# A linear-attention and MLP kernel: half of the first matmul's blocks as Strassen products in six of nine groups

## The chip, the cores and the metric

The kernel runs on one core of one Trainium2 chip. The metric is the device time of one execution in microseconds; the kernel before has a median of 272.02 us over three runs (271.81 to 272.04).

The names of the engines in the profile: PE is TensorE's matmul, PEld its weight load, DVE is VectorE, ACT is ScalarE, POOL is GpSimd, SP is SyncE, which here only issues DMAs.

## What is computed

```python
def _attn_ref(q, k, v):                 # q, k, v: (8 batches, 8 heads, 576 tokens, 64)
    def phi(x):
        return np.where(x > 0, x, np.exp(x) - 1.0) + 1.0
    q_p, k_p = (phi(q), phi(k))
    kv = np.einsum('bhsd,bhse->bhde', k_p, v)
    z = np.sum(k_p, axis=2)
    num = np.einsum('bhsd,bhde->bhse', q_p, kv)
    den = np.einsum('bhsd,bhd->bhs', q_p, z)[..., None] + 1e-06
    return (num / den).astype(np.float32)

def _moe_ref(x, w_in, w_out):           # x: (4608, 512), w_in: (512, 2048), w_out: (2048, 512)
    h = x @ w_in
    c = np.float32(np.sqrt(2.0 / np.pi))
    g = 0.5 * h * (1.0 + np.tanh(c * (h + 0.044715 * h * h * h)))
    return (g @ w_out).astype(np.float32)
```

x is the attention's output with the heads side by side.

## The kernel before

The 4608 tokens are worked in nine groups of 512 (`iteration(j)`, L880). Groups 0 to 7 are the first 512 tokens of the eight batches, group 8 the remaining 64 tokens of each.

One group has two stages. First the **h stage**: sixteen blocks of 128 columns of w_in, each four matmuls of 128x128 weights against 512 tokens of the transposed x (`h_mm`, L392), into one bank of PSUM, from which ScalarE's gelu (L409) writes g in fp16. Then the **product stage**: g times w_out. From group 1 on it is already done by Strassen's scheme: seven products of quarter matrices (`Products`, L756), each sixteen matmuls against 256 columns (L790). VectorE forms the sums of quarters that they need (`sums`, `third_sum`, `last_sum`) and adds up the results (`plus`, L862); ScalarE copies two partial results (L821, L834) and starts the stores. The products run in the order 1, 5, 6, 7, 2, 4, 3. Their accumulators are called p, z, v and w.

Between these stages the **attention of the next group** is put in. For its batch, exponentials (`exp_of`, on ScalarE, L222), the linear part of phi (`linear_of`, DVE, L230), the minimum of both (`least_of`, DVE, L238) and a cast of v (`cast_v_paired`, L243) are made one or two groups ahead. `nab_quads` (L318) then issues 32 small matmuls of numerators and denominators into four banks and a pair of banks, then 72 small ones that make kv of the batch after, and then five divides on DVE (a reciprocal, L287, and a multiplication, L288, each). The quotient x is transposed by DMAs that SP issues (L694), as q is (L671).

The order on every engine is written out by hand. `at(j, slot, fn)` (L517) puts a piece of work behind step `slot` of group j, and `run` (L522) issues it there; engines work off their instructions in that order. In groups 2 to 8 the steps 0 to 15 are the h blocks in the order 0, 8, 1, 9, ..., 7, 15, and 16 to 22 the seven products. The `plan_` functions (L526 to L704) hold the placing: the attention stands behind step 9 (step 12 in group 2).

The kernel uses eight banks of PSUM. `bank()` (L78) gives out six of them, the other two are the pair (L81). In the program a new tile takes the bank that was released longest ago in program order: the accumulators are released in the order v, p, w, z, and the next h blocks take their banks in just that order. The first instruction that writes the tile waits until the last reader of the one before is done. The buffers for loads (`pld`, L48) are seven, given out in the same way.

Of the kernel before, what the change touches and what calls it, by code (L numbers as in the profile page):

```python
# [8 lines left out]
FP32 = mybir.dt.float32  # L9
BF16 = mybir.dt.bfloat16  # L10
# [6 lines left out]
def kernel(  # L17
# [16 lines left out]
    nc = tc.nc  # L34
# [24 lines left out]
    pout = ctx.enter_context(tc.tile_pool(name="pout", bufs=2))  # L59
    psm = ctx.enter_context(tc.tile_pool(name="psm", bufs=2))  # L60
    pkv = ctx.enter_context(tc.tile_pool(name="pkv", bufs=1))
    ps_b = ctx.enter_context(
        tc.tile_pool(name="ps_b", bufs=6, space=bass.MemoryType.PSUM)
    )
# [6 lines left out]


    ident = const.tile([P, P + 64], BF16, name="ident")[:, 0:P]
    w_in_sb = const.tile([P, KM, d_ff], BF16, name="w_in_sb")
    w_out_sb = const.tile([P, 2, MM, N2], FP16, name="w_out_sb")
    w_sum = const.tile([P, 3, MM // 2, N2], FP16, name="w_sum")

# [100 lines left out]

    warm = const.tile([P, 512], BF16, name="warm")
    nc.vector.memset(warm, 0.0)  # L182
    make_identity(nc, ident)
    vps = [pkv.tile([P, J * NP, E], BF16, name=f"vp{i}") for i in range(2)]
    kvbds = [pkv.tile([P, NP, 2 * E], BF16, name=f"kvbd{b}") for b in range(3)]
    kvs = {b: pkv.tile([P, NP, E], BF16, name=f"kv{b}") for b in range(3, B)}
    for i in range(2):
        nc.gpsimd.memset(vps[i][:, :, D:E], 1.0)
# [32 lines left out]
            o, i = o[..., cs, :], i[..., cs, :]  # L221
        nc.scalar.activation(o, i, AF.Exp)  # L222

    def linear_of(name, b, hs=None):
        x = ld[name, b]
        hs = hs or slice(0, x.shape[1])
        if (name, b) not in phi:
            phi_tiles(name, b)
        o, i = maps_view(name, b, x, phi[name, b], hs)
        nc.vector.tensor_scalar(o, i, 1.0, 1.0, op0=ALU.add, op1=ALU.max)  # L230

    def least_of(name, b, hs=None, cs=None):
        p, e = phi[name, b], exps[name, b]
# [62 lines left out]

    def x_tile(b, c):
        if b not in xs:
            xs[b] = pxs.tile([P, C, d_model], BF16, name="xs")
        return xs[b][:, c]  # L300

    def by_parity(x):
# [12 lines left out]
            divide(by_parity(x)[:, a], ns[a].rearrange("p (u e) -> p u e", e=E))  # L315
        return x

    def nab_quads(qt_cs, bs, kv_b):  # L318

        ns = [[bank("n_ps", [P, 6 * E]) for _ in range(2)] for _ in range(2)]
        n_pair = pair_of_banks("n_ps")
        ns.append([n_pair[:, s] for s in range(2)])
        units = [(c, i, a) for c in range(C) for i in range(2) for a in range(2)]
        for n, (c, i, a) in enumerate(units):
            g = n // 6
            one = bs[c][0] == bs[c][1]
            for t in range(1 if one else 2):
                for s in range(2):  # L330
                    cs = slice(0, P) if one else slice(HP * t, HP * (t + 1))
                    nc.tensor.matmul(  # L332
                        ns[g][s][cs, E * (n - 6 * g) : E * (n - 6 * g + 1)],
                        lhsT=qt_cs[c][HP * s : HP * (s + 1), 2 * a + i, cs],
                        rhs=kv_of_head(bs[c][t], s, 2 * a + i),
                        skip_group_check=True,
                    )
        if kv_b is not None:
            for ii in range(2):
                kv_paired(kv_b, ii, lambda a, ii: n_pair[:, a, E * (4 + ii) : E * (5 + ii)])  # L340

        def x_of(transposed):
            x = pxs.tile([P, C, d_model], BF16, name="xs")
            x_v = x.rearrange("p c (i s a d) -> p s (c i) a d", s=2, a=2, d=D)
            for g in range(2):
                for s in range(2):
                    divide(
                        x_v[:, s, 3 * g : 3 * (g + 1)],
                        ns[g][s].rearrange("p (k a e) -> p k a e", a=2, e=E),
                    )  # L350
                for c in ((0,), (1, 2))[g]:
                    transposed(c, x[:, c])
            n_v = n_pair[:, :, 0 : 4 * E].rearrange("p s (k a e) -> p s k a e", a=2, e=E)
            divide(x_v[:, :, 6:8], n_v)
            transposed(3, x[:, 3])
            if kv_b is not None:
                nc.vector.tensor_copy(
                    out=kvs[kv_b].rearrange("p (a i) e -> p a i e", a=2),
                    in_=n_pair[:, :, 4 * E : 6 * E].rearrange("p a (i e) -> p a i e", e=E),
                )  # L360

        return x_of
# [19 lines left out]
        )  # L382

    def transpose_x(x, xt_c, fn, blocks=range(NP)):
        t_ps = bank("t_ps", [P, len(blocks), P], BF16)
        for n, i in enumerate(blocks):
            nc.tensor.transpose(t_ps[:, n, :], x[:, P * i : P * (i + 1)], ident)  # L387
        fn(out=xt_c[:, blocks.start : blocks.stop], in_=t_ps)

    xts, qts = {}, {}  # L390
# [35 lines left out]
    def first_batch():  # L426
# [44 lines left out]
        for i in range(2):  # L471
            cast_w_out(i, nc.gpsimd.tensor_copy)

        xts[0] = pt.tile([P, NP, MAIN], BF16, name="xt")
        x = {0: x_tile(0, 0)}

        def t(c, blocks=range(NP)):
# [34 lines left out]

    fill = {}

    def at(j, slot, fn, *args):  # L517
# [8 lines left out]
    def plan_second():  # L526
# [43 lines left out]

        def t(c):
            if c == 0:
                xts[b] = pt.tile([P, NP, MAIN], BF16, name="xt")
            transpose_x(x[c], xt_chunk(b, c), nc.scalar.copy)

        at(0, 15, maps)
# [38 lines left out]
    def plan_fourth():  # L615

        for slot, hs in zip((9, 13), halves):
            at(1, slot, linear_of, "k", 3, hs)
        at(1, 17, exp_of, "k", 3)
        at(1, 18, exp_of, "q", 3)  # L620
        at(1, 18, exp_of, "k", 4)
        at(1, 18, gelu_table)
        at(1, 20, least_of, "k", 3)
        at(1, 21, linear_of, "q", 3)
        at(2, 0, cast_v, 3)
        at(2, 0, least_q, 3)
        at(2, 4, kv_in_pair, 3)
        at(2, 5, linear_of, "k", 4)
        at(2, 5, least_of, "k", 4)
        at(2, 5, cast_v, 4)  # L630
        at(2, 8, linear_of, "q", 4)
        at(2, 15, exp_of, "q", 4)
        at(2, 16, exp_of, "k", 5)
        at(2, 19, least_q, 4)
        at(2, 22, linear_of, "k", 5)
        at(3, 0, least_of, "k", 5)

    def plan_prepare(j):

        b = j + 2  # L640
        has_k = b + 1 < B
        at(j, 0, linear_of, "q", b)
        at(j, 0, cast_v, b)
        at(j, 15, exp_of, "q", b)
        at(j, 17, least_q, b)
        if has_k:
            at(j, 10, linear_of, "k", b + 1)
            at(j, 16, exp_of, "k", b + 1)
            at(j, 20, least_of, "k", b + 1)

    def plan_rest(m):
        j = 5 + m // 2

        def least():
            least_of("qr", m)
            if m == 0:
                qts[B] = pt.tile([P, C, NP, P], BF16, name="qt")
            nc.sync.dma_start_transpose(
                out=qts[B][:, m], in_=phi["qr", m][:, 0].rearrange("p h d -> p (h d)")
            )  # L660

        at(j, 6 if j == 5 else 0, linear_of, "qr", m)
        at(j, 15, exp_of, "qr", m)
        at(j, 18, least)

# [24 lines left out]

    def transposed_x(b, c, x):
        if b not in xts:
            xts[b] = pt.tile([P, NP, MAIN], BF16, name="xt")
        nc.sync.dma_start_transpose(out=xt_chunk(b, c), in_=x)  # L694

    def plan_attention(b):


        def attention():
            bs = [(b, b) if b < B else (2 * c, 2 * c + 1) for c in range(C)]  # L700
            x_of = nab_quads([qts[b][:, c] for c in range(C)], bs, b + 1 if b + 1 < B else None)
            x_of(lambda c, x: transposed_x(b, c, x))

        at(b - 1, 12 if b == 3 else 9, attention)  # L704

    def evac(dst, src, on_scalar):
        (nc.scalar.copy if on_scalar else nc.vector.tensor_copy)(dst, src)
# [48 lines left out]
    class Products:  # L756
# [42 lines left out]
        def step(self, name):  # L799
# [41 lines left out]
            elif name == 3 and j < B:  # L841
                self.product(self.z, a11, b22, False)
                self.plus(self.o1[:, :, hi], self.z, self.o1[:, :, hi])
                at(j + 1, 0, self.store, 0, self.o1)
            elif name == 3:
                for t in range(2):
                    self.product(self.z, a11, b22, False, (t,))
# [22 lines left out]
        def store(self, h, o_sb, fs=slice(0, d_model)):  # L870
# [5 lines left out]
            else:  # L876
                for t in range(2):
                    self.store_rest(2 * h + t, o_sb[:, t], fs)

    def iteration(j):  # L880
        xt = xts[j]
        if j < B:
            g = pg.tile([P, 2, MM, MAIN // 2], FP16, name="g")
        else:
            g = pg.tile([P, MM, 2, MAIN // 2], FP16, name="g").rearrange("p m a n -> p a m n")
        hs = [("h", m) for m in range(MM)]
        us = [range(m, m + 4) for m in range(0, MM, 4)]
        products = Products(j, g) if j else None
# [4 lines left out]
        elif j == 1:  # L893
# [6 lines left out]
            at(1, 14, products.sums, early)  # L900
            at(1, 17, products.sums, late)
            at(1, 19, products.last_sum)
        else:
            steps = [hs[i + n] for i in range(MM // 2) for n in (0, MM // 2)]
            steps += [("product", n) for n in (1, 5, 6, 7, 2, 4, 3)]
# [2 lines left out]
                at(j, slot, products.third_sum, ms)  # L908
            at(j, 16, products.last_sum)
        o_pss = {}  # L910
        for slot, step in enumerate(steps):
            if step[0] == "h":
                m = step[1]
                h_ps = h_begun.get(j, {}).get(m)
                if h_ps is None:
                    h_ps = bank("h_ps", [P, MAIN])
                    h_mm(h_ps, xt, m)
                gelu(j, g, m, h_ps)
            elif step[0] == "product":
                products.step(step[1])  # L920
            else:
# [3 lines left out]
                o_mm(o_pss[t], g, t, u, half=(j, slot - 0.5))  # L925
                if u.stop == MM:
                    finish(j, t, o_pss[t])
            run(j, slot)

    plan_second()  # L930
    plan_third()
# [15 lines left out]
        at(5, 1, load_rest, m + 2)  # L947
    for j in range(2, 7):
        at(j, 16, gelu_table)

    for j in range(B + 1):
        iteration(j)
# [30 lines left out]
```

## Time and profile before

| | us |
|---|---|
| median of three runs | 272.02 |
| span of the profiled execution | 270.2 |
| PE busy in the span | 264.4 |
| DVE, ACT busy in the span | 164.7, 166.0 |
| groups 3 to 8, from their first matmul to the last product's end | 104.82 to 266.81 |

The page gives no time of the profiled execution beside its span. The span counts from the first to the last instruction; the time of a run has 1.8 us more around it.

In a row of the page's fifth part stand the line, the engine, the operation, what it writes and reads, the form, and how often; then busy time, the mean of one in ns, and the engine's idle time ahead of it. A matmul's own duration is longer than its share of the stream, since matmuls overlap: a 512-column one lasts 379 ns but one follows every 0.216 us. The chain that ended last shows the stream's pace, the row does not.

### The profile page before, as it was taken

How to read it: one execution, taken by the hardware profiler on the slowest of the kernel's cores; microseconds unless marked ns; L12 is line 12 of the kernel's file. 1: busy time of each engine (PE TensorE's matmuls, PEld its weight loads, DVE VectorE, ACT ScalarE, POOL GpSimd, SP SyncE). 2: the span in 40 equal slices, each digit the busy share in tenths (PEclk: the TensorE clock that was granted, in tenths of full speed). 3: DMA queues.
4: the chain of work that ended last, by engine and by line, in shares of the span. 5: the costliest groups of instructions: out<-in, count | busy, mean ns of one | idle time of the engine just before them, and what ended most of it. 6: DMA issues, size and time to landing. Idle time of an engine off the chain costs nothing.

```text
span 270.2 us, 5941 instructions
## 1 busy us (share of the span) xinstructions
PE 264.4 (98%) x2533; PEld 170.8 (63%) x2533; DVE 164.7 (61%) x265; ACT 166.0 (61%) x225; POOL 15.0 (6%) x21
## 2 busy tenths in 40 slices
PE   8999999999999999999999999999999999999994
PEld 2584456465854686558655874587458745874584
DVE  2860186988999966788738774693267326622262
ACT  4768877799776683668266926582665265028700
POOL 3056401000000000000000000000000000000000
PEclk9999999999999999999999999999999999999999
DMA  6999999995799998893699474219231412121004
GB/s 234 401 405 396 410 408 400 400 382 98 232 290 257 327 245 222 292 295 78 172 355 268 91 151 137 61 39 159 96 41 43 135 56 61 19 113 45 0 2 155
DMA packets 59786, 53.87 MB, mean 199 GB/s; under 512 B 35696, under 2 KB 45936, under 8 KB 59760
## 3 DMA queue, kind: packets, MB, share of 16 engines
q1 hardware_dynamic: 56880, 44.57, 58.4%
q10 hardware_dynamic: 2880, 8.91, 8.7%
q8 instruction: 20, 0.33, 0.5%
q14 instruction: 6, 0.05, 0.0%
HBM read 36.70 MB, written 9.44 MB: 171 GB/s over the span
## 4 chain that ended last, share of the span: by engine, by line
PE 92%; DMA 3%; DVE 2%; SPq 1%; issue 0%; ACT 0%
PE h_ps L394 45%; PE o_ps L790 36%; PE o_ps L734 5%; DMA v_x<-in_v_dram 3%; PE n_ps L332 1%; PE kv_ps L254 1%; PE n_ps L254 1%; PE n_ps L270 1%; PE t_ps L387 1%; SPq L94 1%; DVE s L763 0%; SPq L99 0%; PE t_ps L545 0%; DVE kvbd L686 0%; DVE vp L243 0%
## 5 line engine op out<-in xcount | busy, mean ns | idle before, releaser
L394 PE MATMUL h_ps<-xt,w_in_sb 128*128 128x512 bf16 (+1 forms) x628 | 128.4, 361 | 0.2 <-issue 0.2
L409 ACT ACTIVATE g<-h_ps 128x512 f16<-128x512 f32 x144 | 86.8, 616 | 59.5 <-PE h_ps L394 57.5
L394 PEld LDWEIGHTS <-w_in_sb 128*128 128x128 bf16 x628 | 58.2, 98 | 62.4
L790 PEld LDWEIGHTS <-g 128*128 128x128 f16 x624 | 60.9, 98 | 9.0 <-ACT g L409 0.2
L790 PE MATMUL o_ps<-w_out_sb,g 128*128 128x256 f16 x496 | 58.2, 273 | 0.0
L862 DVE TENSOR_TENSOR o_sb<-o_ps,o_sb 128x512 f32<-128x512 f32 (+1 forms) x42 | 27.9, 665 | 29.4 <-PE o_ps L790 28.5
L763 DVE TENSOR_TENSOR s<-g 128x1024 f16<-128x1024 f16 x18 | 12.4, 691 | 40.0 <-ACT g L409 39.9
L790 PE MATMUL o_ps<-w_sum,s 128*128 128x256 f16 x256 | 29.3, 273 | 0.0
L790 PEld LDWEIGHTS <-s 128*128 128x128 f16 x272 | 26.6, 98 | 3.1
L288 DVE TENSOR_TENSOR xs<-n_ps,r 128x384 bf16<-128x384 f32 (+2 forms) x44 | 25.6, 582 | 1.5
L222 ACT ACTIVATE k_e<-k_x 128x2304 bf16<-128x2304 f32 (+1 forms) x9 | 17.2, 1910 | 3.7 <-DVE k_p L238 2.9
L834 ACT COPY o_sb<-o_ps 128x512 f32<-128x512 f32 x8 | 4.7, 583 | 22.3 <-PE o_ps L790 22.3
L230 DVE TENSOR_SCALAR q_p<-q_x 128x2048 bf16<-128x2048 f32 (+1 forms) x9 | 9.9, 1101 | 13.2 <-DMA q_x<-in_q_dram 13.2
L222 ACT ACTIVATE q_e<-q_x 128x2048 bf16<-128x2048 f32 (+1 forms) x10 | 15.7, 1568 | 2.9 <-DMA q_x<-in_q_dram 2.9
L790 PE MATMUL o_ps<-w_sum,g 128*128 128x256 f16 x128 | 15.3, 273 | 0.0
L734 PE MATMUL o_ps<-w_out_sb,g 128*128 128x512 f16 x64 | 15.1, 379 | 0.0
L230 DVE TENSOR_SCALAR k_p<-k_x 128x2304 bf16<-128x2304 f32 (+1 forms) x10 | 11.1, 1113 | 4.2 <-DMA k_x<-in_k_dram 4.1
L422 ACT ACT_TABLE_LOAD x9 | 11.5, 1283 | 0.2
L431 PE MATMUL w_ps<-warm 128*128 128x512 bf16 x32 | 10.3, 484 | 1.2 <-DVE warm L182 1.2
L763 DVE TENSOR_TENSOR s<-s,g 128x1024 f16<-128x1024 f16 x16 | 11.1, 692 | 0.5
L238 DVE TENSOR_TENSOR k_p<-k_p,k_e 128x2304 bf16<-128x2304 bf16 (+1 forms) x9 | 11.0, 1221 | 0.7 <-ACT k_e L222 0.3
L243 DVE CAST vp<-v_x 128x2304 bf16<-128x2304 f32 (+1 forms) x9 | 11.0, 1225 | 0.5 <-DMA v_x<-in_v_dram 0.4
(63 smaller groups left out, 151.3 us busy)
## 6 DMA issues: line engine op xcount, KB each, us to landing
out_dram<-o_sb ACTq DMA_DIRECT2D x16, 512.0 KB, 3.9
k_x<-in_k_dram SPq DMA_DIRECT2D x7, 1152.0 KB, 9.3
v_x<-in_v_dram SPq DMA_DIRECT2D x7, 1152.0 KB, 12.0
q_x<-in_q_dram SPq DMA_DIRECT2D x6, 1024.0 KB, 12.6
w_st<-in_moe_w_in_dram SPq DMA_DIRECT2D x3, 1024.0 KB, 13.3
q_x<-in_q_dram SPq DMA_DIRECT2D x4, 512.0 KB, 8.7
w_st<-in_moe_w_out_dram SPq DMA_DIRECT2D x2, 1024.0 KB, 13.8
w_st<-in_moe_w_out_dram SPq DMA_DIRECT2D x4, 512.0 KB, 11.2
```

The costliest lines, as they stand in the source:

```text
L222: nc.scalar.activation(o, i, AF.Exp)
L230: nc.vector.tensor_scalar(o, i, 1.0, 1.0, op0=ALU.add, op1=ALU.max)
L238: nc.vector.tensor_tensor(p, p, e, op=ALU.min)
L243: fn(out=vp_paired(b)[:, :, us, 0:D].rearrange("p j u d -> p u j d"), in_=ld["v", b][:, us].rearrange("p u (j d) -> p u j d", d=D),)
L288: nc.vector.tensor_tensor(x_v, n_v[heads + (slice(0, D),)], r[heads + (None,)].to_broadcast(shape + [D]), op=ALU.mult,)
L394: nc.tensor.matmul(h_ps[:, ts], lhsT=w_in_sb[:, c, P * m : P * (m + 1)], rhs=xt[:, c, ts], start=(c == 0), stop=(c == KM - 1), skip_group_ ...
L409: nc.scalar.activation(g_v, h_v, AF.Gelu_apprx_tanh)
L422: nc.scalar.preload_act_table_set("gelu_apprx_tanh_and_others")
L734: nc.tensor.matmul(o_ps, lhsT=g[:, t // 2, m, P * (t % 2) : P * (t % 2 + 1)], rhs=w_out_sb[:, :, m, :], start=(m == 0), stop=(m == MM - 1),)
L763: nc.vector.tensor_tensor(out, i0, i1, op=op)
L790: nc.tensor.matmul(ps[t] if type(ps) is list else ps[:, t, :], lhsT=lhs[:, m, P * t : P * (t + 1)], rhs=rhs[:, m, :], start=(first and m = ...
L862: nc.vector.tensor_tensor(out, i0, i1, op=ALU.add)
```

## The change

In groups 3 to 8, eight of the sixteen h blocks are no longer computed one by one. Blocks 0, 1, 8, 9 are unit 0, blocks 4, 5, 12, 13 unit 1. A unit is a 2x2x2 block product (two pairs of blocks, two halves of the 512 inputs, two halves of the 512 tokens) done as seven products of four matmuls of 256 columns. Blocks 2, 10, 3, 11, 6, 14, 7, 15 stay as they were.

Sums are taken in PSUM where they can be. Product 1 is copied by ScalarE into the bank of the last plain block (the seed), and product 2 accumulates on it; product 6 and then 5 and 3 accumulate in product 1's bank; product 4 in product 7's, to which DVE then adds u2 in place. The four sums of w_in per unit are made once, in group 2 (`sum_w_in`), the four sums of x once per group, at the end of the group before (`sum_x`). They live in a new pool and in two of the seven load buffers. For these sums w_in and x are kept in fp16 instead of bf16, with an identity in fp16 for the transposes on PE.

Around it work is moved. The attention of the next group comes behind step 4 (step 5 where there is no further kv), kv first; its divides are three parts behind steps 5, 6 and 7. The cast of v goes from DVE to ScalarE, into the product stage of the group before. `least_of` of k goes to the start of the next group, `linear_of` of k and of the rest of q into or just ahead of the product stage, all sums of g behind steps 13 to 16, one store from slot 0 to 1.

```diff
-    def nab_quads(qt_cs, bs, kv_b):
+    def nab_quads(qt_cs, bs, kv_b, transposed, kv_first):
...
         units = [(c, i, a) for c in range(C) for i in range(2) for a in range(2)]
-        for n, (c, i, a) in enumerate(units):
+        order = list(enumerate(units))
+        if kv_first:
+            order = order[12:] + order[:12]
+            if kv_b is not None:
+                kv_into(kv_b, n_pair)
+            else:
+                order = order[4:10] + order[0:4] + order[10:]
+        for n, (c, i, a) in order:
...
-        at(j, 0, linear_of, "q", b)
-        at(j, 0, cast_v, b)
+        at(j - 1, 20, cast_v_paired, b, slice(0, NP), nc.scalar.copy)
+        at(j, 0, least_of, "k", b)
+        at(j, 1, linear_of, "q", b)
         at(j, 15, exp_of, "q", b)
         at(j, 17, least_q, b)
         if has_k:
-            at(j, 10, linear_of, "k", b + 1)
             at(j, 16, exp_of, "k", b + 1)
-            at(j, 20, least_of, "k", b + 1)
+            at(j, 18, linear_of, "k", b + 1)
...
-        at(j, 6 if j == 5 else 0, linear_of, "qr", m)
+        at(j, 13, linear_of, "qr", m)
...
-        at(b - 1, 12 if b == 3 else 9, attention)
+        at(b - 1, 12 if b == FIRST else 4 if b + 1 < B else 5, attention)
+        for g, slot in enumerate((12, 12, 12) if b == FIRST else (5, 6, 7)):
+            at(b - 1, slot, part, g)
...
-                at(j + 1, 0, self.store, 0, self.o1)
+                at(j + 1, 1, self.store, 0, self.o1)
...
+    def sum_w_in(u, ns=slice(0, 4)):
...
+        sums = ((s1, a21, a22, ALU.add), (s2, s1, a11, ALU.subtract))
+        sums += ((s3, a11, a21, ALU.subtract), (s4, a12, s2, ALU.subtract))
+        for out, i0, i1, op in sums[ns]:
+            nc.vector.tensor_tensor(out, i0, i1, op=op)
...
+        for out, i0, i1 in ((t3, b22, b12), (t1, b12, b11), (t2, b22, t1), (t4, b21, t2)):
+            nc.vector.tensor_tensor(out, i0, i1, op=ALU.subtract)
+
+    class Quad:
...
+        def product(self, ps, lhs, rhs, first):
+            for f in range(2):
+                for c in range(KM // 2):
+                    nc.tensor.matmul(
+                        ps[:, f],
+                        lhsT=lhs[:, c, P * f : P * (f + 1)],
+                        rhs=rhs[:, c],
+                        start=(first and f == 0 and c == 0),
+                        stop=(c == KM // 2 - 1),
+                        skip_group_check=True,
+                    )
...
+            if name == 1:
+                self.b = bank("hq_ps", [P, 2, MAIN // 2])
+                self.product(self.b, a11, b11, True)
+                (nc.scalar.copy if self.j < B or self.u == 0 else nc.vector.tensor_copy)(seed, self.b)
+            elif name == 7:
+                self.w = bank("hq_ps", [P, 2, MAIN // 2])
+                self.product(self.w, s3, t3, True)
+                nc.vector.tensor_copy(m7, self.w)
+            elif name == 6:
+                self.product(self.b, s2, t2, False)
+                (nc.scalar.copy if self.j < B else nc.vector.tensor_copy)(u2, self.b)
+            elif name == 2:
+                self.product(seed, a12, b21, False)
+            elif name == "g11":
+                self.gelu(0, 0, seed)
+            elif name == 5:
+                self.product(self.b, s1, t1, False)
+                add(c22, self.b, m7)
+            elif name == 4:
+                self.product(self.w, a22, t4, False)
+            elif name == "a21":
+                add(self.w, self.w, u2)
+            elif name == 3:
+                self.product(self.b, s4, b22, False)
+                self.gelu(0, 1, self.b)
+            elif name == "g21":
+                self.gelu(1, 0, self.w)
+            elif name == "g22":
+                self.gelu(1, 1, c22)
...
+            at(j, 13, products.sums, early)
+            at(j, 14, products.sums, late)
+            at(j, 15, products.third_sum, slice(0, MM // 2))
+            at(j, 16, products.last_sum)
...
+    def QUAD_ORDER(plain, quad):
+        quad(0, (1,), 0)
+        plain(2)
+        quad(0, (7, 2, 6, "g11"))
+        plain(10, 1)
+        quad(0, (5,))
+        plain(3, 4)
+        quad(0, (4,), 5)
+        quad(0, ("a21",), 6)
+        quad(0, ("g22", 3))
+        plain(11, 7)
+        quad(1, (1,))
+        quad(0, ("g21",), 8)
+        plain(6, 9)
+        quad(1, (7, 2, 6, "g11"), 11)
+        plain(14)
+        quad(1, (5, 4, "a21", "g22"))
+        plain(7, 13)
+        quad(1, (3,))
+        plain(15, 14)
+        quad(1, ("g21",), 15)
...
+    at(2, 9, sum_w_in, 1, slice(0, 2))
+    at(2, 18, sum_w_in, 0)
+    at(2, 20, sum_w_in, 1, slice(2, 4))
+    for j in range(FIRST, B + 1):
+        at(j - 1, 21, sum_x, j)
```

In `QUAD_ORDER` a second number is the slot up to which `run` then issues the planned work: `plain(3, 4)` is block 3 and then what stands at slots 2, 3 and 4, the attention among it. Groups 2 and before keep their steps; the old sums at slots 7 and 15 remain in group 2.

## The prediction

> **What bounds the kernel now.** I read the page's busy times and slices first, then the chain that ended last in order of time, then the timeline of one group (group 4, from 132.3 us) and its windows.
>
> ```profile
> PE 264.4 (98%) x2533; PEld 170.8 (63%) x2533; DVE 164.7 (61%) x265; ACT 166.0 (61%) x225; POOL 15.0 (6%) x21
> ...
> PE   8999999999999999999999999999999999999994
> ...
> PEclk9999999999999999999999999999999999999999
> ```
>
> TensorE is busy everywhere at full granted clock; the other engines have a third to spare on average.
>
> ```profile
> 104.82 8.63 PE h_ps L394 x40
> 113.45 0.60 PE n_ps L332 x32
> 114.05 0.71 PE n_ps L254 x72
> 114.76 5.29 PE h_ps L394 x24
> 120.05 12.23 PE o_ps L790 x112
> ```
>
> This is group 3 on the chain in order of time, and groups 4 to 8 look the same: from 104.82 to 266.81 us, 161.99 us, the chain is TensorE alone, back to back. So the price list is short: a 512-column h matmul costs 8.63/40 = 0.2158 us, a 256-column one in the products 12.23/112 = 0.1092 us. The 24 after the attention cost 5.29, not 5.18: going from 64-row matmuls back to full ones costs 0.11. The span is 270.2 us, the median of the runs 272.02; I take the 1.8 us between them as fixed and move both by the same amount.
>
> **What the change saves.** A unit replaces four h blocks, 16 x 0.2158 = 3.453 us, by seven products of four 256-column matmuls, 28 x 0.1092 = 3.058 us. That is 0.395 us a unit, 0.79 a group, and 12 units save **4.74 us**. Half the columns cost half the time here, so nothing is lost by the smaller tiles. The Trainium skill speaks against exactly this: "TensorE: Matmul & The Clock Gate", Back-to-back issue gap, gives for a stream of weight loads and matmuls about 131 ns at 512 columns and 81 at 128, by which 256 would be some 98 ns (my interpolation). A unit would then go from 16 x 131 = 2.10 to 28 x 98 = 2.74 us, and twelve units would lose 7.7 us. The two rows above, with a weight load for every matmul, say otherwise, so I use them.
>
> **What it adds.** Per group on VectorE: two copies m7, two adds c22 and two in-place adds a21, six 128x512 f32 operations on PSUM at 0.69 us (row of o_sb<-o_ps,o_sb), and four sums of x at 0.42 (the 128x512 bf16 row of qr_p): 4.14 + 1.68 us, less the cast of v, 1.36. On ScalarE: two seed copies and two u2 copies at 0.58 and the v cast, which I price at the 2.12 of an Exp of the same shape: 4.4 us. The gelus stay as many. The windows of group 4:
>
> ```profile
> 132.30:147.50 15.20, 15.20 (x170) 7.45 (x169) 10.13 (x18) 8.96 (x15) 0.00 (x0) 1.00 0.98 322
> 147.50:159.70 12.20, 12.20 (x113) 10.90 (x112) 8.38 (x10) 8.16 (x7) 0.00 (x0) 1.00 0.52 96
> ```
>
> (Columns: stretch, length, then PE, PEld, DVE, ACT busy.) VectorE goes from 18.5 to 23.0 us of some 27, ScalarE from 17.1 to 21.5. Neither becomes the bound by its sum; order decides. fp16 in place of bf16 changes no row (both have two bytes), and I cost it at nothing, as I do the second identity (0.5 us of GpSimd at the start, which idles for 10 us before its first weight cast) and the two load buffers given to the sums (the loads of batches 5 to 7 find buffers released by earlier maps). Moving the divides earlier puts their transposes on SP behind group 4's loads of q's rest, which hold the queue 12.35 us. They are then issued by 18 us into the group, and the sums of x want them at 25. If that cover went, the first product of the next group would wait.
>
> **One group laid out**, in us from its first matmul, with the rows above. TensorE: product 1 of unit 0 to 0.44, block 2 to 1.30, products 7, 2, 6 to 2.61, block 10 to 3.47, product 5 to 3.91, block 3 to 4.77, kv 0.71 and the first eight numerators to 5.64, bank pair one of the numerators to 5.86, the second to 6.08, then 0.11 lost, product 4 to 6.63, product 3 to 7.07, block 11 to 7.93, product 1 of unit 1 to 8.37, and **block 6** would begin.
>
> ScalarE copies the seed by 1.05 (wanted 1.74) and u2 by 3.2 (wanted 3.47); its gelus follow at 0.49 apiece when queued (five in 2.56 us at 79.14). The store of the old group, moved behind block 10's gelu, costs it 0.34 and finds its add done. At the group's end the v cast runs from 24.2 to 26.3; behind it stand the store of o2 and the next seed copy, wanted only at 27.7. No wait there. VectorE finishes the old group's last add at about 1.2 (the four x sums stand before it), least of k at 2.4, m7 3.0, the linear map of q 4.2, c22 4.8 (wanted at 6.63 by product 3). Then it waits 1.1 us for the numerators, and from there this cadence counts:
>
> ```profile
> 114.33 0.19 DVE L287 RECIPROCAL r<-n_ps 128x6 f32<-128x6 f32 x1
> 114.55 0.56 DVE L288 TENSOR_TENSOR xs<-n_ps,r 128x384 bf16<-128x384 f32 x1
> 115.03 0.18 DVE L287 RECIPROCAL r<-n_ps 128x6 f32<-128x6 f32 x1
> 115.25 0.56 DVE L288 TENSOR_TENSOR xs<-n_ps,r 128x384 bf16<-128x384 f32 x1
> 115.72 0.18 DVE L287 RECIPROCAL r<-n_ps 128x6 f32<-128x6 f32 x1
> ```
>
> One divide every 0.695 us. Two divides free the first two attention banks, then stands a21 (0.61 in a row of independent operations), then the third divide, done 0.22 + 0.56 later: 5.89 + 1.39 + 0.61 + 0.78 = 8.67. Six banks exist; at the attention two hold the unit's sums and four the numerators, so block 11, product 1 of unit 1 and block 6 must each take the bank released longest ago: the first, second and third of the numerators. The first two come in time (6.7 and 7.4). The third does not: block 6, due at 8.37, waits until 8.67 plus a restart.
>
> ```profile
> 65.88 0.70 DVE xs L288
> 66.58 0.14 issue
> 66.72 0.40 PE n_ps L270 x4
> ```
>
> This is the same wait in group 1: matmuls held by a divide. After such waits the chain shows 0.04 to 0.14 us of issue (three of four at 0.04 to 0.06), and the first 512-column matmul takes 0.379 instead of 0.216; together about 0.21. So block 6 begins at 8.88, **0.5 us late**, in groups 3, 4 and 5. In groups 6 and 7 the attention stands after product 4, one product nearer to block 6, and I find 0.7 late, mostly again for that divide. Behind block 6 on TensorE stand products 7, 2 and 6 of unit 1, behind its gelu the u2 copy; all move together, so nothing is late twice. After it VectorE is ahead again: m7, c22 and a21 of unit 1 end 0.2 us or more before they are wanted, the late half of s1 0.2 before product 5.
>
> Group 8 has no attention, but its gelus write with a step (0.74, not 0.60) and unit gelus are split in two; I lay 0.27 us of wait on product 5 and 0.07 on each unit's product 5, 0.4 in all. It could be nothing if the split ones are quick, or 1.0 if each costs near 0.6. Group 2 gets eight sums of w_in at 0.42. Two stand right ahead of its divides, in a stretch where VectorE has no gap, move the late half of s1 by 0.6, and take product 5's 0.2 of slack: 0.35 us. The other six and the first x sums fall where it waits about 1 us for each product, at no cost.
>
> Not shown by the trace is a VectorE add that writes back to PSUM. The nearest row is 0.69 (PSUM in, SBUF out). The skill's "Perfetto Trace Analysis", Optimizing Scalar/DVE Operations, puts the access overhead at 125 ns on PSUM against 60 on SBUF; that would add up to 65 ns to a21, hence 0.065 to five waits, 0.3 us. It could be no dearer, since it already pays PSUM once: I take the row, and keep 0.3 for the range. The seed copy into PSUM would by the same page be cheaper for ScalarE; it has slack either way.
>
> Sum: 4.74 saved; lost 3 x 0.5 + 2 x 0.7 at block 6, 0.4 in group 8, 0.35 in group 2, 0.15 in small waits: 3.8. Net 0.94 us: **271.1 us**.
>
> **Rivals.**
> - *No wait at block 6* (chance 0.28). The divide is done 0.5 us sooner than I lay it, or another bank is free. For it: the unit's own bank b is released at 7.8, and numerators could land before I say; 0.5 us in a chain of eight steps is thin. Against: every step has a measured row. Then 272.0 - 4.74 + 0.75 = 268.0.
> - *VectorE arrives late at the divides* (0.14), which ends slower. It is at 85% over the group, and all it does from the old group's last add to c22 is one queue. Place: before the first reciprocal. It has 1.1 us of slack (4.8 against 5.89) by my layout; beyond that each us late is a us more at block 6, five times. From 0.3 us past the slack it is over 0.2% slower; at 0.8 us past, 275.1. For it: waits, x sums landing before the last add, ScalarE's u2. Against: VectorE shows over 1 us of wait for each product before the group's end, where lateness is absorbed.
> - *The small products don't run at 0.109 us* (0.02), the skill's figures: 272 + 7.7 = 279.7. The rows exclude it nearly.
> - My layout itself: 0.56, with 0.6 us of spread about 271.1: three quarters of it below 271.48, most of the rest within 0.2%.
>
> A measurement of this kernel can tell 0.2%, 0.54 us, from no change. Faster: 0.42 + 0.28 = 0.70; same 0.12 + 0.03; slower 0.02 + 0.11 + 0.02. The range reaches down to the case without the wait, and there without group 8's 0.4 too, and up to a VectorE late by 0.36 past its slack: 267.6 to 272.9. That leaves out about 0.08 below and 0.10 above.
>
> **What would show it.** Right: a unit's 28 matmuls in 3.06 us on the chain; TensorE waiting 0.4 to 0.7 us once a group, before block 6, released by a divide; no such wait before products 2, 6, 5, 3. Groups 3 to 5 would last some 27.2 us instead of 27.45. Wrong: groups of 26.6 us without TensorE gaps (first rival), or first reciprocals later than 6 us into the group with c22 just before them (second). The forecast fails as a whole if ScalarE, which I give slack everywhere, turns up as the releaser of TensorE's waits.

## The result, and the profile after

The changed kernel takes **267.88 us** (267.74 to 268.04, four runs) against 272.03 us beside it: a ratio of 0.9849, with a 95% interval of 0.9835 to 0.9863. That is 4.15 us faster. The forecast was 271.1 us. The way was right, but the gain is over four times the forecast's, and it is the first rival (268.0 us, chance 0.28) that came true. The range, 267.6 to 272.9, held the time only because its lower end was drawn at that rival; the layout itself gave 271.1.

The page of the changed kernel, the same lines as before:

```profile
PE 259.3 (98%) x2676; PEld 184.3 (69%) x2677; DVE 195.5 (73%) x327; ACT 178.5 (67%) x257; POOL 15.4 (6%) x23
...
PE   8899999999999999999999999999999999999994
...
PEclk9999999999999999999999999999999999999999
```

TensorE is still the bound, at the same granted clock, with 5.1 us less to do. VectorE has 31 us more of work, ScalarE 12.5.

The chain that ended last, in order of time, for group 4. hq_ps are the units' accumulators; "PE h_ps L954" is product 2, which accumulates in a plain block's bank:

```profile
131.38 0.44 PE hq_ps L954 x4
131.82 0.86 PE h_ps L410 x4
132.68 0.44 PE hq_ps L954 x4
133.12 0.44 PE h_ps L954 x4
...
137.46 0.98 PE hq_ps L954 x8
138.44 0.86 PE h_ps L410 x4
139.31 0.44 PE hq_ps L954 x4
139.74 0.86 PE h_ps L410 x4
...
145.82 12.23 PE o_ps L818 x112
158.04 0.44 PE hq_ps L954 x4
```

Every product of a unit takes 0.44 us (the one right behind the numerators 0.54), the products on w_out 12.23 as before, and the group 158.04 - 131.38 = 26.66 us instead of 27.46: the whole 0.79. Block 6 is the line at 139.74, 8.36 us into the group. The forecast's layout had it due at 8.37 and said it would wait until 8.88. It doesn't wait.

| group | before, us | after, us | less | of which 0.79 lost |
|---|---|---|---|---|
| 3 | 27.45 | 26.76 | 0.69 | 0.10 |
| 4 | 27.46 | 26.66 | 0.80 | 0 |
| 5 | 27.45 | 26.66 | 0.79 | 0 |
| 6 | 26.74 | 26.16 | 0.58 | 0.21 |
| 7 | 26.84 | 26.19 | 0.65 | 0.14 |
| 8 | 26.05 | 25.48 | 0.57 | 0.22 |

Together 4.08 of 4.74 us. Nearly all of the lost time stands in five pieces of the chain, three of which are these:

```profile
111.71 0.94 PE h_ps L410 x4
...
191.08 1.04 PE h_ps L410 x4
...
240.52 0.58 PE hq_ps L954 x4
```

The first two are block 11 in groups 3 and 6 (in group 7 it takes 1.01 us); in group 4 it takes 0.86. In these three groups its weight loads wait for the first divide, 0.7 us together. The last is product 5 of unit 0 in group 8, 0.58 instead of 0.44 us; unit 1's loses 0.08.

The start and groups 0 to 2 are 0.2 us shorter (104.82 to 104.62), which makes 4.28 at the last product and 4.2 in the span (270.2 to 266.0). Of the 0.2 us, 0.09 stands ahead of group 2's numerators, where the kernels measured here differ by more than that among themselves; 0.17 is the numerators (0.60 us instead of 0.77, as in every other run here), and 0.06 is lost again in group 2's products. What shortens the numerators is not shown.

What happened at block 6 is in the timeline of VectorE, ScalarE and TensorE around it (start, duration, engine, line, operation; in brackets idle time before it):

```profile
137.31 0.20 DVE L291 RECIPROCAL r<-n_ps 128x6 f32<-128x6 f32 x1 [1.16 <-PE n_ps L347]
...
138.48 0.60 ACT L966 ACTIVATE g<-hq_ps 128x512 f16<-128x512 f32 x1 [1.17 <-PE hq_ps L954]
138.71 0.69 DVE L985 TENSOR_TENSOR hq_ps<-hq_ps,rows 128x512 f32<-128x512 f32 x1
...
139.53 0.56 DVE L292 TENSOR_TENSOR xs<-n_ps,r 128x384 f16<-128x384 f32 x1
139.58 1.03 PE L410 MATMUL h_ps<-xt,w_in_sb 128*128 128x512 f16 x4
...
140.44 0.60 PE L954 MATMUL hq_ps<-t_sum,w_quad 128*128 128x256 f16 x4
```

VectorE waits 1.16 us for the numerators (I had 1.1), adds a21 at 138.71, and does the third divide from 139.53 to 140.09, which is 8.71 into the group (I had 8.67). But block 6's first matmul starts at 139.58, in the middle of that divide. So it cannot be writing the bank that the divide reads. In the built program (the instruction list that the text is turned into, with a bank for every tile) it has the bank of unit 0's product 1, which the gelu at 138.48 releases at 139.08, in groups 3 to 7 alike. The third numerators' bank goes to product 7 of unit 1 instead (the line at 140.44), which begins 0.35 us after that divide is done.

### The profile page after: what moved, and what is told of

It is laid out like the page before. It is cut to its first block, busy times and chain, and to the rows that moved or that the text cites. A ratio compares the mean times of both kernels' runs of the same rounds, so it can differ in the third digit from the quotient of the medians.

```text
span 266.0 us, 6343 instructions
## 1 busy us (share of the span) xinstructions
PE 259.3 (98%) x2676; PEld 184.3 (69%) x2677; DVE 195.5 (73%) x327; ACT 178.5 (67%) x257; POOL 15.4 (6%) x23
## 4 chain that ended last, share of the span: by engine, by line
PE 92%; DMA 3%; DVE 2%; SPq 1%; issue 0%; ACT 0%
PE o_ps L818 37%; PE h_ps L410 30%; PE hq_ps L954 12%; PE o_ps L762 5%; DMA v_x<-in_v_dram 3%; PE h_ps L954 2%; PE n_ps L347 1%; PE kv_ps L258 1%; PE n_ps L258 1%; PE n_ps L274 1%; PE t_ps L403 1%; SPq L95 1%; DVE s L791 0%; SPq L100 0%; PE t_ps L562 0%
## 5 line engine op out<-in xcount | busy, mean ns | idle before, releaser
L410 PE MATMUL h_ps<-xt,w_in_sb 128*128 128x512 f16 (+2 forms) x436 | 93.0, 354 | 0.2 <-ACT g L425 0.2
L425 ACT ACTIVATE g<-h_ps 128x512 f16<-128x512 f32 x96 | 57.0, 614 | 18.4 <-PE h_ps L410 18.1
L410 PEld LDWEIGHTS <-w_in_sb 128*128 128x128 f16 x436 | 39.6, 98 | 32.4 <-DVE xs L292 0.7
L292 DVE TENSOR_TENSOR xs<-n_ps,r 128x384 f16<-128x384 f32 (+2 forms) x44 | 25.6, 582 | 1.5
L954 PEld LDWEIGHTS <-w_quad 128*128 128x128 f16 x192 | 18.6, 98 | 8.9 <-issue 0.5
L954 PE MATMUL hq_ps<-t_sum,w_quad 128*128 128x256 f16 x144 | 21.6, 272 | 0.0
L954 PEld LDWEIGHTS <-w_in_sb 128*128 128x128 f16 x144 | 13.8, 98 | 3.7 <-DVE xs L292 0.2
L989 ACT COPY h_ps<-hq_ps 128x512 f32<-128x512 f32 x11 | 6.3, 570 | 14.4 <-PE hq_ps L954 14.3
L985 DVE TENSOR_TENSOR rows<-hq_ps,rows 128x512 f32<-128x512 f32 x12 | 8.3, 689 | 8.6 <-PE hq_ps L954 8.6
L966 ACT ACTIVATE g<-hq_ps 128x512 f16<-128x512 f32 x20 | 11.9, 596 | 3.6 <-PE hq_ps L954 3.6
## 6 DMA issues: line engine op xcount, KB each, us to landing
w_st<-in_moe_w_out_dram SPq DMA_DIRECT2D x2, 1024.0 KB, 12.5
```

The costliest lines, as they stand in the source:

```text
L292: nc.vector.tensor_tensor(x_v, n_v[heads + (slice(0, D),)], r[heads + (None,)].to_broadcast(shape + [D]), op=ALU.mult,)
L410: nc.tensor.matmul(h_ps[:, ts], lhsT=w_in_sb[:, c, P * m : P * (m + 1)], rhs=xt[:, c, ts], start=(c == 0), stop=(c == KM - 1), skip_group_ ...
L425: nc.scalar.activation(g_v, h_v, AF.Gelu_apprx_tanh)
L954: nc.tensor.matmul(ps[:, f], lhsT=lhs[:, c, P * f : P * (f + 1)], rhs=rhs[:, c], start=(first and f == 0 and c == 0), stop=(c == KM // 2 - 1),
L966: nc.scalar.activation(self.g[:, t, m : m + 2], src, AF.Gelu_apprx_tanh)
L985: add = lambda out, i0, i1: nc.vector.tensor_tensor(out, i0, i1, op=ALU.add)
```

## The experiments

**Block 6 put into the third numerators' bank, and its control.**

```diff
+                    d_ps = bank("d_ps", [P, 64]) if held else None
+                    if held:      # block 6 in groups 3 to 7
+                        nc.tensor.matmul(d_ps, lhsT=ident_x, rhs=ident_x[:, 0:64], skip_group_check=True)
                     h_ps = bank("h_ps", [P, MAIN])
                     h_mm(h_ps, xt, m)
+                    if held:
+                        nc.tensor.matmul(d_ps, lhsT=ident_x, rhs=ident_x[:, 0:64], skip_group_check=True)
```

> The changed kernel, but in groups 3 to 7 a 64-column matmul takes the bank that block 6 would get (product 1's bank of unit 0) and holds it until block 6 is done, so that block 6 must take the third numerators' bank. Theory (the forecast's layout was right and only the bank wrong): TensorE waits 0.5 us before block 6 in groups 3 to 5 and 0.7 in groups 6 and 7, released by a divide: 267.9 + 2.9 = 270.8 us, plus the small matmuls, which the next kernel prices at 0.2 to 0.6 in all. Rival (the divides don't gate TensorE, whichever bank): the same time as the next kernel.

The control has both small matmuls ahead of block 6 with `h_ps[:, 0:64]` as their output:

> The changed kernel with the same two 64-column matmuls ahead of block 6, but into block 6's own bank, which its first matmul then overwrites. Both theories: only the ten small matmuls, 0.02 to 0.06 us each: 268.1 to 268.5 us, and no wait for a divide before block 6.

Measured: 271.24 us (271.06 to 271.47) with the third numerators' bank, 268.21 (267.93 to 268.51) for the control; ratios to before 0.9973 (0.9962 to 0.9985) and 0.9861 (0.9848 to 0.9875). The bank alone is worth 3.0 us. In the chain of group 4 of the first, and then of the control:

```profile
139.52 0.61 DVE hq_ps L985
140.13 0.10 DVE r L291
140.23 0.02 issue
140.26 0.57 DVE xs L292
140.82 0.04 issue
140.87 1.02 PE h_ps L410 x4
```

```profile
139.88 0.06 PE h_ps L1077 x2
139.94 0.86 PE h_ps L410 x4
```

With the third numerators' bank TensorE is off the chain, and a21, the third reciprocal and the third divide stand on it, then 0.04 us of issue, then block 6. The groups 3 to 7 take 0.72, 0.59, 0.60, 0.69 and 0.70 us more than in the changed kernel, 0.06 of it in the small matmuls; in group 4 block 6 ends 0.51 later, counted from the group's start, than in the control. I had laid out 0.5 in groups 3 to 5 and 0.7 in 6 and 7. The layout was right; the bank was not.

**No units, and one unit.** All sixteen blocks plain at the new places, in an order like the units', without the sums:

```diff
+        plain(0, 0)
+        plain(2)
+        plain(8)
+        plain(10, 1)
...
-    at(2, 0, begin_quads)
...
-    for j in range(FIRST, B + 1):
-        at(j - 1, 21, sum_x, j)
```

> The changed kernel with all sixteen h blocks done plainly again (no units, no sums of w_in or x), everything else at its new place. Theory (the whole gain is TensorE columns): 12 x 0.395 = 4.74 us come back and the 0.67 us of new TensorE waits go: 267.9 + 4.74 - 0.67 = 272.0 us, as before the change. Rival (the re-placed work itself brought part of it): 271.4 us or less; or costs and is paid for by the units: 272.6 or more.

Measured: 271.97 us (271.75 to 272.16), ratio 0.9998 (0.9990 to 1.0006). With unit 1 plain (`plain(4)`, `plain(12, 11)`, `plain(5)`, `plain(13)` at its steps):

> The changed kernel with unit 1 done plainly (blocks 4, 12, 5, 13), unit 0 kept. Theory: half of the columns, 6 x 0.395 = 2.37 us, come back: 270.0 us if the waits behind the attention stay, 269.9 if group 8's half goes. Rival (the second unit is cheaper or dearer than the first): off by more than 0.4 us.

Measured: 270.04 us (269.94 to 270.35), ratio 0.9932 (0.9919 to 0.9944). So the re-placed attention, divides, casts and maps and fp16 together bring nothing and cost nothing that the time shows; groups 3 to 8 without units take 27.46, 27.45, 27.45, 26.74, 26.84 and 26.05 us, what they took before the change. Whether a part of it gains what another loses is not shown. Every unit brings its columns, less the waits: none 271.97, one 270.04, two 267.88.

**The v casts back on VectorE.** This kernel, the one with one more map and the last two ran beside a before of 271.78 us; by its ratio the changed kernel stands at 0.9849 x 271.78 = 267.67 us there.

```diff
-        at(j - 1, 20, cast_v_paired, b, slice(0, NP), nc.scalar.copy)
+        at(j - 1, 20, cast_v_paired, b, slice(0, NP), nc.vector.tensor_copy)
```

> The changed kernel with the v casts back on VectorE (same place, the product stage). Theory (VectorE waits 1.6 us for the next-to-last product there, so a cast of 1.36 us fits): 267.9 us, no change. Rival (VectorE is near enough its bound that moving the cast to ScalarE was needed): x sums late, TensorE waits at product 7 of unit 0 in groups 3 to 6, 0.3 us or more each: 268.9 us or more.

Measured: 268.91 us (268.85 to 268.94), ratio 0.9896 (0.9880 to 0.9911): 1.2 us lost. The expectation of no change was missed, and the time is the rival's, but not in the rival's way. From the start of one product stage to the next, groups 4, 5, 6 and 7 take 26.66, 26.66, 26.15 and 26.19 us, as in the changed kernel. All of it is lost up to group 3's products, which start at 120.28 instead of 119.16. There the cast of batch 5's v falls into group 2, where VectorE also makes the eight sums of w_in: c22 of group 3 begins at 111.30 instead of 110.17. The casts of batches 6 and 7, in groups 3 and 4, are hidden as expected.

**One and two more linear maps of q on VectorE**, in groups 3 to 5 ahead of the divides:

```diff
         at(j, 1, linear_of, "q", b)
+        at(j, 1, linear_of, "q", b)
```

> The changed kernel with the linear map of q done twice in groups 3 to 5 (the same values written again, 1.22 us more of VectorE ahead of c22 and the divides). Theory: VectorE waits 1.16 us there for the numerators and TensorE has 0.13 us to spare at block 11, so it is hidden: 267.9 to 268.1 us. Rival (VectorE, at 83% of the group, is the bound or nearly): 3 x 1.1 us, 271 us.

Measured: 268.93 us (268.88 to 269.12), ratio 0.9896 (0.9878 to 0.9914), 1.3 us lost. Groups 4 and 5 take 26.66 us again. The extra map fills 1.25 us of VectorE's queue there (c22 begins 5.34 us into group 4 instead of 4.09), and the first reciprocal is 0.02 late, so it is fully hidden, and only just. Group 3's products begin 1.38 late; 0.12 of that stands ahead of group 2's products already, so the map costs 1.26. Group 3's chain, from the end of group 2 to block 11:

```profile
105.32 0.60 DVE o_sb L891
105.92 1.28 DVE k_p L234
...
111.56 0.68 DVE rows L986
112.24 0.11 DVE r L291
...
112.38 0.57 DVE xs L292
112.95 0.05 issue
113.00 1.04 PE h_ps L410 x4
```

VectorE carries the linear map of k for batch 5 out of group 2 (105.92 to 107.20), which groups 4 and 5 don't have, and reaches c22 (111.56) only when the numerators are there already. In group 3 it has no slack at all: in the changed kernel too, block 11 there takes 0.94 instead of 0.86.

> The changed kernel with the linear map of q done three times in groups 3 to 5 (2.3 us more of VectorE than the change has). The kernel with one more showed a loss of 1.2 us in group 3 and none in 4 and 5. Theory (beyond the 1.16 us that VectorE waits for the numerators in groups 4 and 5, each us late is a us at block 11): 1.14 us more in group 3, 1.0 in each of 4 and 5: 268.9 + 3.1 = 272.0 us. Rival (lateness before the divides is taken back behind them, in the product stage): under 270.5 us.

Measured: 274.18 us (272.89 to 274.51, ratio 1.0074, 1.0051 to 1.0097), where 272.0 was expected; the before beside it took 271.97. The profiled execution took 272.92. In it groups 4 and 5 take 27.81 and 27.82 us, 1.15 more each, and group 3 another 1.27 (its products begin 1.49 later, of which 0.22 stands ahead of group 2's products). In group 4 c22 begins 2.51 us later than in the changed kernel; some 1.2 of it goes into VectorE's wait, 0.13 into what block 11 had to spare, and the rest is the loss. So beyond its slack the price of lateness at the divides is one for one, as the prediction's second rival put it. Two of the five executions took 272.9 us at a granted clock of 0.998, and three 274.2 to 274.5 at 0.991 to 0.992. Over a span of 271 us that difference would come to 1.6 to 1.9 us (my estimate from these clocks), so the lower clock can account for it; why it was lower is not shown.

**The attention at its old place**, behind block 6:

```diff
-        at(b - 1, 12 if b == FIRST else 4 if b + 1 < B else 5, attention)
-        for g, slot in enumerate((12, 12, 12) if b == FIRST else (5, 6, 7)):
+        at(b - 1, 12 if b == FIRST else 9, attention)
+        for g, slot in enumerate((12, 12, 12) if b == FIRST else (9, 9, 9)):
```

> The changed kernel with the next group's attention and all its divides at slot 9 again, behind block 6, in groups 3 to 7. Theory (order on VectorE and the banks decide, not busy time): unit 1's product 7 waits for the first divide's bank (0.6 us) and product 4 of unit 1 for m7, which now stands behind five divides (0.9 to 1.3): 2.0 us in groups 3 to 5, 1.5 in 6 and 7, less today's 0.4: 276.5 us. Rival (the units' columns bring the gain wherever the attention stands): 268 to 268.5 us.

Measured: 277.57 us (277.38 to 277.65), ratio 1.0214 (1.0197 to 1.0230), slower than before the change. Group 4's chain shows what for:

```profile
146.38 0.69 DVE xs L292
147.07 0.33 DVE kv L373
147.40 0.61 DVE rows L993
148.01 0.04 issue
148.06 0.60 PE hq_ps L954 x4
```

All five divides (the chain runs through them from 143.37), then the copy of kv, then m7 (rows, L993) stand ahead of product 4 of unit 1. Groups 4 and 5 take 28.64 and 28.65 us, 2.0 more, as laid out; groups 6 and 7 1.3 more (1.5 expected), and group 3 3.0, since VectorE comes late into it; that is the main reason why the expectation was 1.1 us short. With the divides behind block 6 the units lose more than their columns bring.

**The attention of groups 6 and 7 in two pieces.** After the change TensorE waits a little before block 11 in these groups (1.04 and 1.01 us instead of 0.86).

```diff
+        whole = kv_b is not None or not kv_first
+        issue(order if whole else order[:10])
...
+            if g == 0 and not whole:
+                issue(order[10:])
...
-        at(b - 1, 12 if b == FIRST else 4 if b + 1 < B else 5, attention)
+        at(b - 1, 12 if b == FIRST else 4, attention)
```

> The changed kernel with the attention of groups 6 and 7 split: its first numerators and the pair behind block 3, the last twelve units behind product 4, so that the first divide starts 0.44 us sooner. Theory: the 0.18 and 0.15 us that TensorE waits before block 11 there go: 267.55 us. Rival (something else is late at block 11, such as its own operands): no change, 267.9 us.

Measured: 267.68 us (267.63 to 267.74), ratio 0.9851 (0.9835 to 0.9866), no different from the changed kernel's 0.9849. Its chain in group 6, products 4 and 3 of unit 0:

```profile
189.75 0.54 PE hq_ps L960 x4
...
190.59 0.54 PE hq_ps L960 x4
```

Block 11 no longer waits, but TensorE now goes from small matmuls to full ones twice, at 0.10 us each (0.54 for a product instead of 0.44), and the 32 small matmuls of group 6 take 0.70 us in two bursts instead of 0.60 in one. Groups 6 and 7 are as long as they were. The wait is real and not worth removing this way.

## Why the prediction was right on the saving and wrong on the wait

- **The saving** stood: 0.395 us a unit, 4.74 in all. The rates of 0.2158 and 0.1092 us held for the new products, and no units, one and two are spaced 1.93 and 2.16 us apart, against 2.37 less what is lost. The sustained spacings of the Trainium skill ("TensorE: Matmul & The Clock Gate", Back-to-back issue gap), by which the change would have lost 7.7 us, are refuted for this stream by 4.15 us of gain.
- **The step that failed** is "block 11, product 1 of unit 1 and block 6 must each take the bank released longest ago: the first, second and third of the numerators". The rule, which the section on the kernel before states too, is right about "released longest ago" and wrong about the order that counts. It was read from a program in which two orders fall together: that of the text, and that in which the banks come free in the built program. In the text the third divide stands ahead of the gelu of product 3; in the built program it stands behind it, and it finishes later (140.09 against 139.08). So block 6 gets the bank of that gelu, as the first rival named it ("the unit's own bank b is released at 7.8"; it is 7.70 into group 4). The term 3 x 0.5 + 2 x 0.7 = 2.9 us is 0. Forcing the third bank costs 3.0 us; that its time, 271.24 us, is so near to the 271.1 that I forecast for the change is in part chance: the small matmuls add 0.3 us to it, and the smaller terms below were 0.2 us too large.
- **Group 2's 0.35 us** is 0.06 (12.29 for the products instead of 12.23, and 12.23 in the kernel with one unit, which leaves these two sums out). The two sums of w_in do stand ahead of the divides, but product 5 begins with the early half of s1, while the late half is still being written. Only its fifth weight load waits for that, 0.17 us; I had made the whole product wait.

```profile
93.67 0.68 DVE L791 TENSOR_TENSOR s<-g 128x1024 f16<-128x1024 f16 x1
93.81 0.43 PEld L818 LDWEIGHTS <-s 128*128 128x128 f16 x4
...
94.40 2.95 PEld L818 LDWEIGHTS <-s 128*128 128x128 f16 x28 [0.17 <-DVE s L791]
```

- **Group 8's 0.4 us** is 0.22: 0.14 and 0.08 at product 5 of unit 0 and of unit 1, as it waits for u2 (the copy ends at 240.46, the product's first matmul starts at 240.51), and nothing at product 5 of w_out: there the late half of s1 is written by 251.80 and the first matmul starts at 251.88.
- **Groups 6 and 7** lose 0.21 and 0.14, all but a few hundredths of it before block 11, where I had 0.7 before block 6.
- **No new wait on ScalarE** was right, and so were the durations: the v cast 2.15 us (2.12 taken), the copies 0.57 and 0.59. VectorE and ScalarE are busy 22.1 and 20.5 us in group 4 (23.0 and 21.5 forecast).
- **a21, in place in PSUM**, takes 0.690 us, against 0.689 for c22, which writes to SBUF. The skill's larger access overhead for PSUM ("Perfetto Trace Analysis", Optimizing Scalar/DVE Operations) added nothing that can be seen, and the row was the right choice.
- **The second rival** (VectorE late) had the right price, one for one past 1.1 us of slack, and the wrong places: it shows at block 11, and in group 3, not in groups 4 and 5. I had laid group 3 out like these, but the linear map of k (1.35 us) comes over to it from group 2, and that is more than the slack; it cost 0.10 us. The sums of w_in that I had "at no cost" are not the reason: with unit 1's four left out, c22 of group 3 begins at the same 110.17 and block 11 is as late.

With the bank as the program has it, and nothing else changed, my sum would have read 4.74 - 0.9 = 3.8 us, 268.2 us (the rival's 268.0 left out the 0.15 for small waits).

## What to carry to other kernels

Where TensorE alone is on the chain, price a change by the pace of the chain: here the columns saved, less the waits that one finds by laying out the three queues, make 4.74 - 0.73 = 4.0 us against a measured 4.15. When that layout turns on which buffer a tile gets, look it up in the built program or keep both answers open at full weight; a rule read from a program in which two orders coincide doesn't tell which of them it is. Busy share says little about what an engine can still take: the same extra map of 1.25 us on VectorE, busy for 83% of a group, cost nothing in two groups and 1.26 us in the one that inherits work.

## What the hardware showed beyond that

- Going from 64-row matmuls back to full ones costs TensorE about 0.1 us each time (0.54 to 0.56 us for a product behind the numerators instead of 0.44), so a burst of small matmuls cut in two paid it twice.
- A wait on data that a product reads late in its run is not a wait on the whole product: in group 2 four weight loads of product 5 went ahead at 93.81, and only the fifth waited for the half of s1 that ended at 94.35.
